# One fused attention and two MoE layers on one core: the first six weight blocks converted one VectorE stage per pair, in place of whole steps in six pairs

## The chip, the cores and the metric

The kernel runs on one core of a Trainium2 chip. The metric is the device time of one execution in microseconds (us), the median of three runs. A profile of one further execution gives a time for every instruction. Engine names are those of the profile: PE is TensorE's matmuls, PEld its weight loads, DVE is VectorE, ACT is ScalarE, POOL is GpSimd, SP is SyncE, which here issues most of the DMAs.

## The reference

```python
x = attention(q, k, v, f)        # 4 batches x 8 heads, 576 positions, 64 wide, causal, decay from log f
x = x.transpose(0, 2, 1, 3).reshape(2304, 512)
h = x @ w_in                     # 512 -> 2048
x = (maximum(h, 0) + log1p(exp(-abs(h)))) @ w_out        # softplus, 2048 -> 512
gate = 1 / (1 + exp(-(x @ w_gate)))                      # 512 -> 1536
out = (gate * (x @ w_val)) @ w_out2                      # 1536 -> 512
```

All numbers go in and come out in 32 bits. The weights lie in memory as 64-bit words (doubles), and the kernel makes of each block of 128x512 words two tiles, a high and a low part, which together carry the 32-bit value through the matmuls.

## The kernel before, in words

Attention comes first. The 32 heads are worked two at a time, so there are 16 **pairs**, 0 to 15. For each pair PE makes nine tiles of scores (L209, L220) in PSUM; DVE adds the mask and finds each row's extreme ("minimum", L227), which frees the scores' PSUM; ACT takes the exponential (L232); PE transposes the result through PSUM tiles `t` (L250); ACT copies the high part of each `t` tile out (`evac_h`, L268) and DVE the low part (`evac_l`, L272), which frees the tile; PE multiplies with the values (L322); ACT and DVE take the sums out (L332, L337), and POOL scales them (L340). POOL also splits the next queries, keys and values into high and low parts (L160, L168: `Xh`, `Yh`, `Xl`, `Yl`, `V`). DVE makes the reciprocal of each pair's row sums (L278, L279), PE turns it (`rt`, L284).

There are two `t` tiles and two score tiles `s`, used in turn. The groups of transposes of a pair follow each other on PE in the order 0, 1, 2, 3, `rt`, 5, 4, 6, and then the next pair's 0, each in the `t` tile that the last but one group left. So group 2 waits for `evac_l` of group 0, group 3 for that of group 1, group 5 for that of group 3, the next pair's group 0 for that of group 4, and its group 1 for that of group 6.

No scheduler orders this. Tables give each operation a time in units of the pair's period of 9 (`WHEN`, and `START` and `END` for the first and the last pair); pair p's operations stand at 9p + that number, all are sorted, and each engine's instructions are issued in that order. Every engine works its own queue in order and waits by semaphores.

Between attention's operations the same list takes in other work (`others`). For the weights a class `Weights` converts the blocks one after the other, each through seven stages: LOAD (SP starts a DMA of 512 KB into one of four `raw` tiles, L463), SCALE (ACT, L471), SHIFT, LOW and SIGN (DVE, L485, L487, L489, each over 128x512 32-bit words in SBUF), HI (ACT, L476), LO (POOL, L479). `op(s)` issues stage s for the next block that is ready for it, `tick()` all seven, in the order SCALE, HI, LO, SHIFT, LOW, SIGN, LOAD. During attention's pairs 0 to 15 `limit` allows six blocks, 0 to 5; the other 26 follow from attention's end on, in the next layer.

Before the change `TICKS` puts eight whole ticks among the pairs. The second to the seventh (at -7.81, 1.03, 20.49, 29.25, 38.24 and 47.34) each issue SHIFT, LOW and SIGN of one block, one straight behind the other on DVE; the last issues HI and LO of block 5.

Of the kernel before, what the change touches and what calls it, by code (L numbers as in the profile page):

```python
# [21 lines left out]
class Attention:  # L22
# [13 lines left out]
    def pools(self, pool, io_pool):  # L36
        self.vp = pool("at_v", 2)
        self.pp = pool("at_p", 2)
        self.sm = pool("at_small", 3)
        self.xp = pool("at_x", 2)  # L40
        self.io = io_pool("at_io", 2)
# [663 lines left out]
class Moe2:  # L705
# [53 lines left out]
    STEPS = 10  # L759
# [176 lines left out]

TICKS = [-79.5479, -7.81, 1.0296, 20.4876, 29.246, 38.239, 47.3352, 87.6118]
LATE_TICKS = [-7.39, 35.9211, 42.3787, 45.7979, 60.2136, 64.0078, 68.4722, 70.489, 70.7365, 71.6392, 73.755, 76.4625, 83.1312, 92.4907, 95.2063, 99.2562, 116.366, 144.939, 153.168, 159.446, 198.508]  # L940
X_STEPS = [-50.0345, -24.888, -24.7421, -11.1038, -4.6076, -2.1888, 2.7229, 20.2706]
UNITS = [58.5061, 83.1125]
# [3 lines left out]
def kernel(ctx: ExitStack, tc, q, k, v, f, w_in, w_out, w_gate, w_val, w2_out, out):  # L946
# [18 lines left out]
    W = Weights(nc, stage, 4)  # L965
# [10 lines left out]
    with ExitStack() as actx:  # L976
        ioctx = ExitStack()
        right = pools(actx, side="right")
        at = Attention(nc, q, k, v, f, xT, right, ps, dr)
        at.pools(right, pools(ioctx, side="right"))  # L980
        at.begin()
        end = at.PERIOD * at.NP
        m1 = []

        def open_pools():
            ioctx.close()
            chain = pool("chain", 1, **later)
            wb = pool("wb", 1, **later)
            W.add_slots(wb, tags("b", 2 * MORE))
            W.limit = EARLY + MORE  # L990
            m1.extend([chain, Moe1(nc, FC1, x1, yT, W, chain, ps)])

        others = [(t, W.tick) for t in TICKS] + [(end + t, W.tick) for t in LATE_TICKS]
        others += [(end + t, lambda k=k: x1.step(0, k)) for k, t in enumerate(X_STEPS)]
        others += [(end - .5, open_pools)]
        others += [(end + t, lambda u=u: m1[1].unit(u, 0)) for u, t in enumerate(UNITS)]
        at.run(others)
# [131 lines left out]
```

## Time and profile before

| what | value |
|---|---|
| time, median of three runs | 1063.03 us (1062.92 to 1065.11) |
| time of the profiled execution | 1063.44 us |
| its span, first to last instruction | 1061.7 us |
| PE busy, of the span | 1027.5 us |
| DVE busy, of the span | 678.9 us |
| ACT busy, of the span | 455.2 us |
| POOL busy, of the span | 155.4 us |

The span is what the trace shows; 1.74 us of the execution's time lie around it. Attention takes the first 230 us or so, the two layers behind it the rest. Busy times are sums over the whole span, and a busy PE isn't one at its peak: which engine sets the pace of a stretch is read from that stretch.

### The profile page before, as it was taken

The numbers are of one execution on the slowest core, as the hardware profiler recorded it, in microseconds if no ns is written. First come the engines' busy times: TensorE is split into PE (matmuls) and PEld (weight loads), VectorE is DVE, ScalarE is ACT, GpSimd is POOL, SyncE is SP. The second block draws the span as 40 slices with busy tenths as digits, with TensorE's granted clock in tenths as the row PEclk, the third lists the DMA queues.
The fourth block names the chain that finished last, engine by engine and source line by source line (L and its number), as shares of the span: only waits on it lengthen the run. The fifth ranks groups of instructions, "written<-read, shape, count | busy, mean of one in ns | idle before, by whom it ended". The sixth has DMA issues, their size and how long they took to land.

```text
span 1061.7 us, 17894 instructions
## 1 busy us (share of the span) xinstructions
PE 1027.5 (97%) x6376; PEld 924.9 (87%) x6376; DVE 678.9 (64%) x1453; ACT 455.2 (43%) x989; POOL 155.4 (15%) x158
## 2 busy tenths in 40 slices
PE   4989999989999999999999999999999999999998
PEld 3767888878889999999999998999999999899997
DVE  5899999978955755745755556655655656555421
ACT  4678888866644434344343442222222222221121
POOL 7656777440000000000000000000000000000000
PEclk9999999999999999999999999999999999999999
DMA  6354454445534565564563599997887886686481
GB/s 167 94 151 128 130 145 125 130 138 183 188 128 172 197 233 178 192 236 170 193 225 126 201 358 362 341 314 248 279 262 231 288 261 230 228 296 215 141 274 63
DMA packets 129492, 218.23 MB, mean 206 GB/s; under 512 B 16174, under 2 KB 46526, under 8 KB 129404
## 3 DMA queue, kind: packets, MB, share of 16 engines
q1 hardware_dynamic: 126364, 212.08, 61.0%
q10 hardware_dynamic: 3040, 5.01, 1.4%
q8 instruction: 50, 0.82, 0.3%
q14 instruction: 38, 0.31, 0.1%
HBM read 171.21 MB, written 45.83 MB: 204 GB/s over the span
## 4 chain that ended last, share of the span: by engine, by line
PE 88%; DVE 7%; ACT 2%; issue 1%; DMA 1%; POOL 0%; ACTq 0%; SPq 0%; DVEq 0%; POOLq 0%
PE h L540 7%; PE h L541 7%; PE h L539 7%; PE s L220 5%; PE h_S L541 4%; PE h_S L539 4%; PE h_S L540 4%; PE x L322 4%; PE t L250 4%; PE h_A L539 3%; PE h_A L541 3%; PE h_A L540 3%; PE zX L900 3%; PE zX L901 2%; PE zX L902 2%; PE oY L540 2%
## 5 line engine op out<-in xcount | busy, mean ns | idle before, releaser
L541 PE MATMUL h<-xh,wi_l 128*128 128x448 f32 (+1 forms) x320 | 118.4, 370 | 0.0
L540 PE MATMUL h<-xl,wi_h 128*128 128x448 f32 (+1 forms) x320 | 118.4, 370 | 0.0
L539 PE MATMUL h<-xh,wi_h 128*128 128x448 f32 (+1 forms) x320 | 118.4, 370 | 0.0
L581 DVE TENSOR_TENSOR gl<-L,gh 128x448 fp32r<-128x448 f32 (+1 forms) x80 | 50.9, 637 | 99.4 <-ACT gh L580 88.5
L876 ACT CAST gh<-bl 128x512 fp32r<-128x512 f32 (+1 forms) x60 | 34.6, 579 | 168.6 <-DVE bl L847 141.5
L569 ACT ACTIVATE L<-h 128x448 f32<-128x448 f32 (+1 forms) x80 | 44.2, 552 | 142.3 <-PE h L541 131.1
L232 ACT ACTIVATE P<-P,m 128x128 f32<-128x128 f32 (+3 forms) x144 | 83.4, 583 | 13.1 <-DVE m L227 13.1
L540 PE MATMUL h_S<-x,ring 128*128 128x256 f32 x288 | 81.5, 283 | 0.0
L227 DVE CUSTOM_DVE_ANT_0 P<-s,mask 128x256 f32<-128x256 f32 (+3 forms) x144 | 70.7, 517 | 15.5 <-PE s L220 10.5
L539 PE MATMUL h_S<-x,ring 128*128 128x256 f32 x264 | 74.7, 283 | 0.0
L541 PE MATMUL h_S<-x,ring 128*128 128x256 f32 x264 | 74.7, 283 | 0.0
L250 PE MATMUL t<-ident,P 128*128 128x128 f32 x400 | 62.6, 293 | 7.0 <-DVE PTbl L272 4.0
L541 PEld LDWEIGHTS h<-xh,wi_l 128*128 128x128 f32 x320 | 60.1, 188 | 6.3
L539 PEld LDWEIGHTS h<-xh,wi_h 128*128 128x128 f32 x320 | 60.1, 188 | 6.3
L540 PEld LDWEIGHTS h<-xl,wi_h 128*128 128x128 f32 x320 | 60.1, 188 | 6.3
L250 PEld LDWEIGHTS t<-ident,P 128*128 128x128 f32 x400 | 47.0, 148 | 19.7 <-DVE PTbl L272 5.7
L845 ACT ACTIVATE bh<-bh 128x1024 f32<-128x1024 f32 x24 | 25.4, 1060 | 89.4 <-DVE bh L843 89.4
L681 DVE TENSOR_TENSOR l<-fw,sh 128x512 fp32r<-128x512 f32 x60 | 40.7, 686 | 35.8 <-ACT sh L680 35.7
L540 PEld LDWEIGHTS h_S<-x,ring 128*128 128x128 f32 x288 | 55.3, 192 | 0.0
L833 DVE TENSOR_TENSOR L<-h_S,L 128x256 f32<-128x256 f32 x48 | 20.3, 423 | 53.3 <-PE h_S L541 49.9
L540 PE MATMUL h_A<-x,ring 128*128 128x256 f32 x192 | 54.3, 283 | 0.0
L877 DVE TENSOR_TENSOR gl<-bl,gh 128x512 fp32r<-128x512 f32 (+1 forms) x60 | 38.0, 635 | 24.9 <-ACT gh L876 24.9
(233 smaller groups left out, 3079.5 us busy)
## 6 DMA issues: line engine op xcount, KB each, us to landing
ring<-sd_g SPq DMA_DIRECT2D x192, 256.0 KB
ring<-sd_v SPq DMA_DIRECT2D x192, 256.0 KB
raw_wi<-in_moe_w_in_dram SPq DMA_DIRECT2D x16, 512.0 KB
raw_wo<-in_moe_w_out_dram SPq DMA_DIRECT2D x16, 512.0 KB
fraw<-in_moe_w_gate_dram SPq DMA_DIRECT2D x12, 512.0 KB
fraw<-in_moe_w_out_dram SPq DMA_DIRECT2D x12, 512.0 KB
sd_g<-sh SPq DMA_DIRECT2D x24, 256.0 KB
sd_g<-l SPq DMA_DIRECT2D x24, 256.0 KB
```

Of the source, the lines that this page charges most:

```text
L220: nc.tensor.matmul(ps[h][:, 0:N], L[o], r[o, 0:N], start=j == 0, stop=j == n - 1)
L227: self.nc.vector.tensor_tensor_reduce(P, src, mask, -0.125, 3e38, op0=ALU.add, op1=ALU.min, accum_out=R["m"][:, t:t + 1])
L232: self.nc.scalar.activation(P, P, AF.Exp, bias=R["m"][:, t:t + 1], scale=-1.0, accum_out=R["sum"][:, t:t + 1])
L250: nc.tensor.transpose(ps[:, 128 * n:128 * n + 128], R["P"][:, o:o + 128], self.ident)
L322: nc.tensor.matmul(R["acc%d" % h][:, o:o + n], v, t[:, col:col + n], start=j == 0 and w == 0, stop=j == 1 and w == 1)
L539: nc.tensor.matmul(ps, ah, bh, start=start and i == 0, stop=False)
L540: nc.tensor.matmul(ps, ah, bl, start=False, stop=False)
L541: nc.tensor.matmul(ps, al, bh, start=False, stop=stop and i == n - 1)
L569: nc.scalar.activation(g, ph, AF.Softplus)
L581: nc.vector.tensor_sub(gl, s, gh)
L681: nc.vector.tensor_sub(l, w[n], h)
L877: nc.vector.tensor_sub(l, s, h)
```

## The change

The eight ticks among the pairs go; in their place stand 44 single stages of the same six blocks. The late ticks, from 144 - 7.39 on, stay as they are, and each finds the same blocks done as before.

```diff
-TICKS = [-79.5479, -7.81, 1.0296, 20.4876, 29.246, 38.239, 47.3352, 87.6118]
+STEPS = [(-7.81, 0), (1.294, 1), (3.294, 2), (12.294, 3), (14.294, 0), (21.294, 4), (22.794, 5), (24.294, 6),
+         (28.294, 1), (30.294, 2), (39.294, 3), (41.294, 0), (48.294, 4), (49.794, 5), (51.294, 6), (55.294, 1),
+         (57.294, 2), (66.294, 3), (68.294, 0), (75.294, 4), (76.794, 5), (78.294, 6), (82.294, 1), (84.294, 2),
+         (86.294, 0), (87.381, 3), (93.294, 4), (94.794, 5), (96.294, 6), (100.294, 1), (102.294, 2),
+         (104.294, 0), (105.381, 3), (111.294, 4), (112.794, 5), (114.294, 6), (118, 0), (118.294, 1),
+         (120.294, 2), (123.381, 3), (129.294, 4), (130.794, 5), (132.294, 6), (133, 0)]
...
-        others = [(t, W.tick) for t in TICKS] + [(end + t, W.tick) for t in LATE_TICKS]
+        others = [(t, lambda k=k: W.op(k)) for t, k in STEPS] + [(end + t, W.tick) for t in LATE_TICKS]
```

The second number of a step is the stage: 0 LOAD, 1 SCALE, 2 SHIFT, 3 LOW, 4 SIGN, 5 HI, 6 LO. Worked through in order, the steps put SHIFT of block 0 into pair 0, LOW into pair 1, SIGN into pair 2, SHIFT of block 1 into pair 3, and so on: one DVE stage in each of pairs 0 to 14, always at 9p + 3.294, right behind the minimum of tiles 1 and 7. From block 3 on a block has two pairs and not three, so its LOW stands as a second DVE stage at 9p + 6.381 of pairs 9, 11 and 13. SCALE stands in pairs 0, 3, 6, 9, 11 and 13, HI and LO in pairs 2, 5, 8, 10, 12 and 14.

On DVE, in pair 2, ahead of the minimum of tiles 0 and 8, the kernel before has a whole tick (`w_wi` and `w_wo` are a block's words, `raw` its loaded doubles, the two rows of tiles `s_1` the minimum of tiles 1 and 7, `t_2` and `t_3` the transposed groups 2 and 3):

```order
L272 TENSOR_TENSOR PTal_168<-t_1_478,PTah_167 128x512
L485 TENSOR_SCALAR w_wi_532<-w_wi_532 128x512
L487 SCALAR_TENSOR_TENSOR w_wi_532<-raw_wi_316,w_wi_532 128x512
L489 SCALAR_TENSOR_TENSOR w_wi_532<-raw_wi_316,w_wi_532 128x512
L227 ISA P_437,m_438<-s_1_0_519,mask 128x256
L227 ISA m_438 128x1
L227 ISA P_437,m_438<-s_1_1_520,mask 128x256
L227 ISA m_438 128x1
L272 TENSOR_TENSOR PTbl<-t_2_550,PTbh 128x512
L272 TENSOR_TENSOR PTbl<-t_3_557,PTbh 128x2x256
```

The same place of the changed kernel:

```order
L272 TENSOR_TENSOR PTal_168<-t_1_466,PTah_167 128x512
L227 ISA P_425,m_426<-s_1_0_507,mask 128x256
L227 ISA m_426 128x1
L227 ISA P_425,m_426<-s_1_1_508,mask 128x256
L227 ISA m_426 128x1
L489 SCALAR_TENSOR_TENSOR w_wi_300<-raw_wi_255,w_wi_300 128x512
L272 TENSOR_TENSOR PTbl<-t_2_527,PTbh 128x512
L272 TENSOR_TENSOR PTbl<-t_3_535,PTbh 128x2x256
```

The tick's three stages ahead of the minimum are gone; one stage, SIGN of an older block, stands behind it, ahead of `evac_l` of groups 2 and 3.

On DVE, in pair 9, around the minimum of tiles 6 and 2 (`s_2`) and `evac_l` of groups 5 and 4 (`t_5`, `t_4`), the kernel before has no stage:

```order
L227 ISA P_1806,m_1807<-s_2_1_1978,mask 128x384
L227 ISA m_1807 128x1
L272 TENSOR_TENSOR PTbl<-t_5_1965,PTbh 128x2x256
L227 ISA P_1806,m_1807<-s_2_0_1977,mask 128x384
L227 ISA m_1807 128x1
L272 TENSOR_TENSOR PTbl<-t_4_1972,PTbh 128x384
```

The same place of the changed kernel:

```order
L227 ISA P_1775,m_1776<-s_2_1_1954,mask 128x384
L227 ISA m_1776 128x1
L272 TENSOR_TENSOR PTbl<-t_5_1939,PTbh 128x2x256
L227 ISA P_1775,m_1776<-s_2_0_1953,mask 128x384
L227 ISA m_1776 128x1
L487 SCALAR_TENSOR_TENSOR w_wo_1864<-raw_wo_1559,w_wo_1864 128x512
L272 TENSOR_TENSOR PTbl<-t_4_1946,PTbh 128x384
```

LOW of block 3 has come in ahead of `evac_l` of group 4; pairs 11 and 13 read alike.

## Rows read from the trace of the kernel before

**Rows 1.** The chain of work that ended last, pieces in order: start, us, what.

```profile
48.21 1.49 PE t L250 x7
...
62.71 0.98 PE t L250 x7
...
77.18 1.62 PE t L250 x7
...
92.82 0.98 PE t L250 x7
...
104.52 0.89 PE t L250 x7
...
116.16 0.89 PE t L250 x7
```

**Rows 2.** Busy time by stretch: a pair without a tick, one with block 5's LO.

```profile
115.90:127.50 11.60, 11.60 (x97) 9.78 (x96) 10.69 (x30) 10.09 (x30) 7.93 (x7) 1.00 0.46 128
...
139.10:150.70 11.60, 11.60 (x97) 9.78 (x96) 10.15 (x30) 10.51 (x31) 8.64 (x8) 1.00 0.55 150
```

**Rows 3.** Timeline of DVE, the tick in pair 2: start, us, instruction, idle before.

```profile
42.23 1.29 DVE L485 TENSOR_SCALAR w_wi<-w_wi 128x512 uint32<-128x512 uint32 x1
43.56 1.65 DVE L487 SCALAR_TENSOR_TENSOR w_wi<-raw_wi,w_wi 128x512 uint32<-128x512 uint32 x1
45.24 0.69 DVE L489 SCALAR_TENSOR_TENSOR w_wi<-raw_wi,w_wi 128x512 uint32<-128x512 uint32 x1
```

**Rows 4.** Timeline of POOL, the same stretch.

```profile
41.67 1.57 POOL L168 TENSOR_TENSOR V<-vr,V 128x640 fp32r<-128x640 f32 x1
43.19 1.48 POOL L479 TENSOR_TENSOR wo_l<-w_wo,wo_h 128x512 fp32r<-128x512 f32 x1
```

**Rows 5.** All instructions of line L485: count, ns min/median/max, starts.

```profile
L485 DVE TENSOR_SCALAR w_wi<-w_wi x16: 414/422/1498, 21.0 to 300.0; 128x512 uint32<-128x512 uint32 x16
```

**Rows 6.** Timeline of ACT, first pair: the first copy out of a transposed group.

```profile
22.31 0.59 ACT L268 CAST PTbh<-t 128x512 fp32r<-128x512 f32 x1 [0.29 <-PE t L250]
```

**Rows 7.** Timeline of PE, first and second pair: idle before, and what ended it.

```profile
25.82 1.97 PE L250 MATMUL t<-ident,P 128*128 128x128 f32 x8 [2.69 <-DVE PTbl L272]
...
46.33 0.92 PE L220 MATMUL s<-Yh,Xh 64*128 64x256 f32 x2 [1.74 <-DVE m L227]
```

**Rows 8.** Timeline of DVE, first pairs: `evac_l` behind the second tick, the next minimum.

```profile
29.55 0.68 DVE L272 TENSOR_TENSOR PTal<-t,PTah 128x512 fp32r<-128x512 f32 x1
...
30.75 0.74 DVE L227 CUSTOM_DVE_ANT_0 P<-s,mask 128x576 f32<-128x576 f32 x1
```

**Rows 9.** Timeline of DVE, a pair without a tick.

```profile
107.94 0.56 DVE L272 TENSOR_TENSOR PTbl<-t,PTbh 128x384 fp32r<-128x384 f32 x1
...
111.01 0.94 DVE L278 TENSOR_SCALAR r<-sum 128x9 f32<-128x9 f32 x1
...
114.50 1.29 DVE L272 TENSOR_TENSOR PTbl<-t,PTbh 128x512 fp32r<-128x512 f32 x2 [0.44 <-ACT PTbh L268]
```

**Rows 10.** Timeline of POOL, the same pair.

```profile
107.57 1.58 POOL L168 TENSOR_TENSOR Xl<-qr,Xh 128x640 fp32r<-128x640 f32 x1
...
112.69 1.56 POOL L168 TENSOR_TENSOR V<-vr,V 128x640 fp32r<-128x640 f32 x1
```

**Rows 11.** Timeline of PE, the same pair.

```profile
109.68 1.09 PE L250 MATMUL t<-ident,P 128*128 128x128 f32 x8
...
115.88 0.28 PE L284 MATMUL rt<-ident,r 128*9 128x128 f32 x1
```

**Rows 12.** Timeline of DVE, a later pair: a long reciprocal step.

```profile
192.37 1.35 DVE L278 TENSOR_SCALAR r<-sum 128x9 f32<-128x9 f32 x1
```

**Rows 13.** The chain again: groups 2 and 3, a plain pair's, then the later pair's.

```profile
171.26 1.02 PE t L250 x8
...
194.61 1.20 PE t L250 x8
```

**Rows 14.** Busy time by stretch: PE, PEld, DVE, ACT, POOL, then the granted clock.

```profile
77.40:80.80 3.40, 3.40 (x17) 2.63 (x16) 1.92 (x5) 2.81 (x9) 0.64 (x1) 0.50 0.46 95
```

## The prediction

> **What bounds the kernel now.** The page's totals call PE busy nearly throughout, but they average over stages, so I went to the chain of work in order of time. In attention it meets the same spot once per pair, the seven transposes of groups 5 and 4. Their starts are 48.21, 62.71, 77.18, 92.82, 104.52 and 116.16 [rows 1], so the pairs take 14.50, 14.47, 15.64, 11.70 and 11.64 us. The three long ones hold a tick each. The busy times of a pair without one say what sets its pace: PE 11.60 of 11.60 us, DVE 10.69, ACT 10.09, POOL 7.93 [rows 2]. So a plain pair is PE's, and DVE has 0.91 us to spare in it.
>
> A tick does not fit into that. Its three DVE stages take 1.29 + 1.65 + 0.69 = 3.63 us [rows 3]; less the 0.91 that leaves 2.7, and the pairs show 14.50 - 11.64 = 2.86. In a tick's pair DVE sets the pace and PE waits. The pair of 15.64 holds something more: from 77.40 on, for 3.4 us, the granted clock is 0.50 [rows 14], the lower of the two levels, 1.2 GHz; at half rate 3.4 us do the work of 1.7.
>
> Why does a tick take 3.63? SIGN, when POOL is idle, takes 0.69 [rows 3], and the median of all SHIFTs is 0.42 [rows 5]. In the tick, POOL's split of V ends at 41.67 + 1.57 = 43.24 and SHIFT at 43.52; POOL's LO ends at 44.67 and LOW at 45.21 [rows 3, 4]. So a stage that meets a POOL instruction waits for it and is done 0.28 (SHIFT) or 0.54 (LOW, SIGN) behind its end.
>
> The Trainium skill has this as a rule ("SBUF — State Buffer", section "Who interferes with whom"): VectorE and GpSimd share a pair of ports under an exclusive lock, and an instruction that needs the pair while the other engine holds it waits for the whole of that other instruction. The trace agrees: the 0.28 and 0.54 us are counted from the end of POOL's instruction. As an estimate by that rule, a LOW that comes just as POOL's split of the queries begins would cost the split and itself, 1.58 + 0.69 = 2.3 us [rows 3, 10], where the tick's LOW shows 1.65; for the three second LOWs the gain below would be about 2 us smaller. The rule speaks against the second LOW and hardly against the first slot, where POOL is nearly done.
>
> **The change, part by part.** All of it lies in attention, whose end I take to move with its pairs.
>
> *Removed, startup.* Two ticks stand ahead of the first pair's end. PE waits 2.69 us for the first `evac_l` and goes on at 25.82 [rows 7]. ACT's copy ahead of that `evac_l` is done at 22.31 + 0.59 = 22.90 [rows 6]; with the 0.68 that an `evac_l` takes here [rows 8], PE could start near 23.6, 2.2 us sooner. The second tick holds the next `evac_l` to 29.55, and the minimum behind it to 30.75 [rows 8]; 2.2 sooner on PE and no tick on DVE would let that minimum run at about 27.6, 3.1 sooner. PE and DVE then wait for each other, so I take 2.6, between 2.2 and 3.1.
>
> *Removed, the tick in pair 2.* PE waits 1.74 for the minimum behind it [rows 7]; a later tick costs 2.86. I take 2.4, between these.
>
> *Removed, three ticks more.* 14.50 + 14.47 + 15.64 + 11.70 less four times 11.64 is 9.8 us [rows 1]. That takes in the slow clock. Gains: 2.6 + 2.4 + 9.8 = **14.8** (13.7 to 15.7).
>
> *Added, LOW or SIGN in the slot at 3.294* (pairs 1, 2, 4, 5, 7, 8, 10, 12, 14). DVE comes free at 114.50 - 0.44 = 114.06 and then waits for ACT [rows 9]; this wait is the cover. POOL's split of V runs to 112.69 + 1.56 = 114.25 [rows 10], so the stage ends at 114.79 and `evac_l` of groups 2 and 3 starts up to 0.29 late, about 0.2 as instructions on DVE overlap a little. Behind it hangs PE: that `evac_l` ends at 115.79 and `rt` starts at 115.88 [rows 9, 11], 0.09 apart, and PE has nothing to spare. Nine times 0.2 is 1.8; from 0, if the 0.09 and what POOL does a little sooner cover it, to 0.4 each, 3.6, as pair 14 follows the tables of the end.
>
> *Added, SHIFT in the slot* (pairs 0, 3, 6, 9, 11, 13). It ends at 114.25 + 0.28 = 114.53, in time. But five of these pairs follow one with LO, 1.48 on POOL [rows 4], which pushes POOL's work later, and the reciprocal's first step, which waits for POOL too: one of 1.35 instead of 0.94 [rows 9, 12] made groups 2 and 3 take 1.20 instead of 1.02 [rows 13]. SHIFT itself meets the late split. I take 0.3 each, 1.5; from 0, since the pair with block 5's LO still took 11.60 [rows 2], to 0.6 each, 3.0.
>
> *Added, a second LOW* (pairs 9, 11, 13), ahead of `evac_l` of group 4, which starts at 107.94 [rows 9]. POOL's split of the queries runs from 107.57 to 109.15 [rows 10], so LOW ends at 109.69, and that `evac_l` at 110.2 instead of 108.50. PE wants its tile at 109.68 for the next pair's group 0 [rows 11]. What is late next is group 6's `evac_l`, behind another minimum, and with it group 1. DVE's account of such a pair is 10.69 + 0.42 + 1.7 = 12.8 against 11.60, 1.2 over; with the late LO I take 1.3, so 3.9 in all. The low end is 0.5 each, if the reciprocal's step then finds POOL between two instructions; the high end 2.4, if it meets the whole split of V, 1.56 [rows 10]. That is 1.5 to 7.2.
>
> *Costed at nothing.* ACT's SCALE and HI: ACT has 1.51 us to spare per pair, and the pair with HI of block 5, at 10.51 of ACT, still took 11.60 [rows 2]; without that cover each costs its own length, which lies in the 0.6 above. The LOADs: each stands at least 9 units, one pair, ahead of its SCALE, and its buffer came free pairs before, so SP does not wait at them, nor do the loads of q, k and v that queue behind; LOAD of blocks 6 and 7 moves late, to 118 and 133, but is wanted at 144 + 35.9.
>
> Costs: 1.8 + 1.5 + 3.9 = **7.2**. Sum: 14.8 - 7.2 = 7.6 us. The profiled span of 1061.7 becomes 1054.1; that execution took 1063.44, within 0.04% of the median, so the median becomes 1063.0 - 7.6 = **1055.4 us**, its own range 1052 to 1058.5 (chance 0.50).
>
> **The rivals.** *The late pairs hide the stages* (0.20): 10.69 + 0.69 = 11.38 is still under 11.60, so counted by engine a single stage is free, and only the second LOWs cost, 1.5 to 3. That gives a gain of 12 to 13.5, about 1050.3. Against it: the 0.09 us between `evac_l` and `rt`.
>
> *Every stage is held* (0.17): all three costs near their high ends, 3.6 + 3.0 + 6 = 12.6, because POOL, once late, stays late. Gain 2.2, about 1060.8. For it: every stage of the ticks but SIGN met POOL. Against it: POOL has 3.7 us to spare per pair.
>
> *The gain is given back at attention's end* (0.07): if the last pairs or the next layer's first weights are set by loads and not by PE, the earlier end turns into a wait; 1063. Against it: the order from 144 - 7.39 on is unchanged.
>
> *Slower, by the clock* (0.06). The short waits now fall into all pairs up to 14. If each lowers the granted clock as behind the tick at 77.40, that is 1.7 us apiece [rows 14]. It decides from five such pairs on (5 x 1.7 = 8.5 against 7.6); ten of them give 1063.0 - 7.6 + 17 = 1072. Against it: that drop lies in a tick's pair, whose waits add up to 2.9 us; of the new ones most are 0.2 and three 1.3.
>
> **How the numbers follow.** The range 1049.5 to 1061.0 takes in the main case, most of the first rival and of the second, and leaves out some 0.18. A measurement here can tell about 0.2%, 2.1 us. Faster by more: main, first rival, most of the second, 0.84; within it: the gain given back and the rest of the second, 0.09; slower 0.07, the clock and what I haven't thought of.
>
> **What would show it.** The starts of the same transposes should lie 11.6 to 12.0 apart in pairs with one stage, 12.8 to 13.2 in the three with two. LOW behind the minimum of tiles 6 and 2 should take 1.6 to 1.7 us, SHIFT in its slot under 0.7. The startup should put the first `rt` about 2.6 us sooner. The prediction is wrong if single-stage pairs stay at 11.6 to the hundredth (first rival), if they go past 12.2 (second), if the granted clock falls in late pairs, or if attention ends sooner and the end doesn't.

## The result, and the profile after

The changed kernel takes **1055.0 us** (median of 4 runs, 1051.7 to 1056.0), the kernel before, run beside it, 1063.2 (1062.9 to 1065.1): a ratio of 0.9899, 95% interval 0.9872 to 0.9926. In two later comparisons the medians were 1053.9 and 1053.1 us, the ratios 0.9904 (0.9878 to 0.9929) and 0.9890 (0.9859 to 0.9921). The profiled execution took 1055.97 us, with a span of 1054.2 us. Forecast were 1055.4 us, in a range of 1049.5 to 1061.0.

The first thing to look at is again the chain of work, at the seven transposes of groups 5 and 4, once per pair (start, us, what; compare [rows 1]):

```profile
42.77 0.98 PE t L250 x7
...
54.70 0.95 PE t L250 x7
...
66.37 0.90 PE t L250 x7
...
78.00 0.90 PE t L250 x7
...
89.86 0.89 PE t L250 x7
...
101.49 0.90 PE t L250 x7
...
113.11 0.92 PE t L250 x7
...
124.95 0.89 PE t L250 x7
...
137.77 0.89 PE t L250 x7
```

The long pairs of before (14.50, 14.47, 15.64 us) are gone: the fourth start is 78.00, where before it was 92.82. From there the pairs take 11.86, 11.63, 11.62, 11.84 and 12.82. The last one holds two stages. `rt` (L284), which stands just ahead, gives the same picture for every kernel, so all experiments below are measured by its 16 starts:

| us | before | after |
|---|---|---|
| first `rt` | 39.0 | 36.1 |
| intervals 1 to 5 | 8.84, 14.34, 14.47, 15.64, 11.96 | 6.21, 12.13, 11.68, 11.63, 11.86 |
| intervals 6 to 10 | 11.64, 11.60, 11.60, 11.60, 11.60 | 11.62, 11.63, 11.84, 12.82, 11.84 |
| intervals 11 to 15 | 11.60, 11.72, 11.81, 11.23, 11.10 | 12.77, 12.17, 12.02, 11.53, 11.10 |
| last `rt` | 219.7 | 208.9 |
| from there to the end of the span | 842.0 | 845.3 |

An interval here is the time from one `rt` to the next. Attention ends 10.8 us sooner and the kernel only 7.5 us: 3.3 us are lost behind attention. That is the first puzzle. The second is inside attention, where the new costs are smaller than forecast.

By stretch (PE, PEld, DVE, ACT, POOL, granted clock, DMA share, GB/s; compare [rows 2]) three intervals of the changed kernel, one with SHIFT behind an LO, one with LOW alone, one with two stages:

```profile
77.67:89.56 11.89, 11.85 (x98) 9.80 (x94) 11.60 (x32) 11.10 (x32) 9.21 (x8) 1.00 0.46 134
89.56:101.18 11.62, 11.62 (x96) 9.83 (x94) 11.29 (x32) 10.10 (x30) 7.94 (x7) 1.00 0.53 148
...
124.67:137.49 12.82, 11.88 (x96) 9.80 (x95) 12.64 (x33) 10.21 (x30) 8.38 (x7) 1.00 0.57 156
```

In the second PE is busy for all of 11.62 us: a single stage is hidden. In the last DVE is busy for 12.64 of 12.82 us: DVE sets that pair's pace, PE waits.

The startup, timeline of PE (idle before, and what ended it; compare [rows 7]):

```profile
23.66 1.97 PE L250 MATMUL t<-ident,P 128*128 128x128 f32 x8 [0.55 <-DVE PTbl L272]
...
30.84 0.73 PE L220 MATMUL s<-Yh,Xh 64*128 64x256 f32 x2 [0.51 <-DVE m L227]
```

The first wait has fallen from 2.69 to 0.55 us, and PE goes on at 23.66, 2.2 us sooner, as worked out (23.6). How soon the first `rt` comes varies from execution to execution, though: from 34.7 to 37.0 us in the seven profiles that have the changed startup, from 38.8 to 39.6 in the five that have the one before.

The slot with LOW, timeline of DVE, and of PE at `rt` behind it (compare [rows 9, 11]):

```profile
99.32 0.82 DVE L487 SCALAR_TENSOR_TENSOR w_wi<-raw_wi,w_wi 128x512 uint32<-128x512 uint32 x1
...
100.07 1.27 DVE L272 TENSOR_TENSOR PTbl<-t,PTbh 128x512 fp32r<-128x512 f32 x2
...
101.21 0.28 PE L284 MATMUL rt<-ident,r 128*9 128x128 f32 x1
```

LOW is held a little by POOL (0.82 instead of 0.69), yet `rt` waits for nothing. It starts at 101.21 while the second of the two `evac_l` still runs (to 101.34): it hangs on the first alone.

The pair with SHIFT, timelines of POOL and DVE (compare [rows 9, 10]):

```profile
78.90 1.30 POOL L479 TENSOR_TENSOR wo_l<-w_wo,wo_h 128x512 fp32r<-128x512 f32 x1 [2.79 <-ACT wo_h L476]
80.17 0.73 POOL L160 TENSOR_SCALAR Xh<-qr 128x640 fp32r<-128x640 f32 x1
...
84.41 1.45 POOL L340 TENSOR_TENSOR xs<-xs,rb 128x576 f32<-128x576 f32 x1
...
91.58 0.73 POOL L160 TENSOR_SCALAR Xh<-qr 128x640 fp32r<-128x640 f32 x1 [3.39 <-PE s L220]
...
84.47 1.42 DVE L278 TENSOR_SCALAR r<-sum 128x9 f32<-128x9 f32 x1
```

POOL's LO ends as Xh starts: Xh comes 2.45 us behind `rt` (77.72), where in the interval without LO it comes 1.99 behind (91.58 against 89.59). POOL is some 0.46 late from there on, and L278 is held to the end of POOL's `xs` (85.89 and 85.86): 1.42 us instead of 0.94.

The second LOW of pair 9, timelines of DVE, POOL and PE:

```profile
128.37 1.76 DVE L487 SCALAR_TENSOR_TENSOR w_wo<-raw_wo,w_wo 128x512 uint32<-128x512 uint32 x1
...
128.00 1.58 POOL L168 TENSOR_TENSOR Xl<-qr,Xh 128x640 fp32r<-128x640 f32 x1
129.53 1.87 POOL L168 TENSOR_TENSOR Yl<-kr,Yh 128x576 fp32r<-128x576 f32 x1
...
130.74 0.63 PE L250 MATMUL t<-ident,P 128*128 128x128 f32 x4 [0.58 <-DVE PTbl L272]
131.72 0.66 PE L250 MATMUL t<-ident,P 128*128 128x128 f32 x4 [0.35 <-DVE PTbl L272]
```

LOW meets POOL's split of the queries and ends 0.55 us behind it; PE's transposes wait 0.58 and 0.35 us for the evictions behind LOW.

### The profile page after: what moved, and what is told of

Read it like the earlier page. It is cut to its first block, busy times and chain, and to the rows that moved or that the text cites. A ratio compares the mean times of both kernels' runs of the same rounds, so it can differ in the third digit from the quotient of the medians.

```text
span 1054.2 us, 17893 instructions
## 1 busy us (share of the span) xinstructions
PE 1027.0 (97%) x6376; PEld 920.4 (87%) x6376; DVE 672.3 (64%) x1453; ACT 454.8 (43%) x989; POOL 154.8 (15%) x158
## 4 chain that ended last, share of the span: by engine, by line
PE 91%; DVE 5%; ACT 2%; issue 1%; DMA 0%; POOL 0%; ACTq 0%; SPq 0%; DVEq 0%; POOLq 0%
PE h L541 7%; PE h L540 7%; PE h L539 7%; PE s L220 5%; PE t L250 4%; PE x L322 4%; PE h_S L541 4%; PE h_S L539 4%; PE h_S L540 4%; PE h_A L539 3%; PE h_A L541 3%; PE h_A L540 3%; PE oY L541 3%; PE oY L540 3%; PE oY L539 3%; PE zX L900 3%
## 5 line engine op out<-in xcount | busy, mean ns | idle before, releaser
L581 DVE TENSOR_TENSOR gl<-L,gh 128x448 fp32r<-128x448 f32 (+1 forms) x80 | 51.0, 638 | 104.9 <-ACT gh L580 104.8
L876 ACT CAST gh<-bl 128x512 fp32r<-128x512 f32 (+1 forms) x60 | 34.7, 580 | 168.9 <-DVE bl L847 141.8
L250 PEld LDWEIGHTS t<-ident,P 128*128 128x128 f32 x400 | 44.7, 144 | 21.5 <-DVE PTbl L272 5.2
```

The costliest lines, as they stand in the source:

```text
L250: nc.tensor.transpose(ps[:, 128 * n:128 * n + 128], R["P"][:, o:o + 128], self.ident)
L581: nc.vector.tensor_sub(gl, s, gh)
```

## The experiments

Two theories of the smaller costs stood against each other. *Place*: a stage costs what POOL makes of it and what cover its place has. *Count*: a stage in a full pair costs its own length wherever it stands. And for the 3.3 us lost behind attention: something that differs from execution to execution, or an effect of the change.

**The two kernels unchanged, once more** (three runs, no edit).

> The changed kernel once more, nothing edited. Theory: attention is 11.2 us shorter than in the kernel before in every execution (start of rt15 near 209 us against 219.7), and what varies from execution to execution is the pace of the 448-column matmuls of the first MoE (202.7 or 206.7 ns apart, token tile by token tile, about 1.5 us a tile). Then times lie between 1051.5 (no slow tile) and 1056.2 us (three), and the profiled execution's time goes with its number of slow tiles. Rival: the slow pace comes with the change, by how the weights or the tiles lie in time after it; then tiles 2, 3 and 4 are at 206.7 ns again in this profile and the median is 1055 to 1056 us.

> The kernel before once more, nothing edited. Theory (the pace of the first MoE's matmuls is a state of the execution): a profile of it can show tiles at 206.7 ns too, and its times spread over 1062.9 to about 1067 us; the attention part is equal to the first profile's within 0.2 us. Rival (the slow pace belongs to the change): every tile is at 202.7 ns and the time stays at 1062.9 to 1063.5 us.

> The changed kernel once more, nothing edited, beside the improved one. Both theories of the improved kernel need its time on this chip: 1052 to 1056 us median, attention's intervals as in its two earlier profiles within 0.1 us, and again some token tiles of the first MoE at 206.7 ns a matmul, others at 202.7. If the slow pace belonged to the change and not to the execution, the same tiles as in the first profile (2, 3 and 4) would be slow.

The first MoE works the 2304 positions in token tiles, one of 512 and four of 448, with 384 matmuls each. The matmuls of the 448-column tiles start either 202.7 or 206.7 ns apart. By stretch, 60 us of such a tile each: the changed kernel's first profile (both stretches at 206.7), then its third (202.7), then the second profile of the kernel before (202.7, then 206.7):

```profile
380.00:440.00 60.00, 60.00 (x292) 54.49 (x291) 35.37 (x65) 24.79 (x45) 0.00 (x0) 1.00 0.55 188
...
540.00:600.00 60.00, 60.00 (x292) 54.49 (x292) 31.18 (x57) 24.42 (x45) 0.00 (x0) 1.00 0.47 161
```

```profile
540.00:600.00 60.00, 60.00 (x298) 55.61 (x297) 32.84 (x62) 25.50 (x47) 0.00 (x0) 1.00 0.50 172
```

```profile
380.00:440.00 60.00, 60.00 (x298) 55.59 (x297) 34.80 (x63) 25.68 (x47) 0.00 (x0) 1.00 0.57 198
460.00:520.00 60.00, 60.00 (x293) 54.48 (x292) 33.76 (x61) 24.86 (x45) 0.00 (x0) 1.00 0.58 202
```

With DVE, ACT and DMA about equally busy and the clock granted in full, a 60 us stretch holds 298 matmuls or some 292. Once slow, the stream stays slow for the rest of these tiles (but the last 12 matmuls, which come 5 us behind the others). The changed kernel had some three tiles, one and none at the slow pace in its three profiles; the kernel before none and two. From the last `rt` to the end the changed kernel took 845.3 us with three and 841.3 with none: 4.0 us, 1.3 a tile. (With one it took 844.1; there the granted clock was 0.50 for 6.8 us from 209.6 on, too.) So the slow pace needs no change, and the change doesn't always bring it: it belongs to the execution. Of all twelve profiles nine show it, six of the eight with single stages and three of the four without. With no slow tile the changed kernel took 1050.6 us.

Where the pace changes can be read from the traces: always at one of three places, near matmul 313, 697 or 1081 of the 1536, some four fifths into a tile, where PE's weight load waits for DVE's low part `gl` (L581). In the changed kernel's first profile, timeline of PEld:

```profile
368.19 0.19 PEld L540 LDWEIGHTS oX<-gl,wo_h 128*128 128x128 f32 x1 [0.29 <-DVE gl L581]
```

At other times the same wait passes and the pace stays. Why it changes at one and not at another is open.

Attention is reproduced: from first to last `rt` 172.8, 173.2 and 172.8 us in the changed kernel, 180.7 and 180.4 in the one before. The times spread further than the slow tiles were expected to spread them: the changed kernel's from 1051.0 to 1058.5 us (expected 1051.5 to 1056.2), the kernel before's up to 1071 (expected 1067). The start of the first `rt` is one thing more that varies; and the kernel before's second profile holds, beside those at 77.4 and 220.8, one more stretch at the lower clock, at 647 us.

**The second LOW earlier, behind the `xs` operations** (DVE's, L337, which take the sums out).

```
-(86.294, 0), (87.381, 3), ... (104.294, 0), (105.381, 3), ... (123.381, 3)
+(86.294, 0), (86.3, 3),   ... (104.294, 0), (104.3, 3),   ... (122.3, 3)
```

> The changed kernel with the second LOW of pairs 9, 11 and 13 issued some 1.6 us earlier, right behind the two xs operations of VectorE, before GpSimd's Xl and Yl start. Theory: those two pairs take 12.8 us because the stage is held by GpSimd (1.76 us instead of 0.69) and then holds the transposes; issued ahead of GpSimd's Xl it takes 0.7 to 0.8 us and the two pairs fall from 12.8 to about 11.9 us each; attention ends 1.5 to 2 us earlier and the median goes from 1055 to about 1053.3 us. Rival: VectorE has no slack between minimum 6 and the transposes' eviction, so that any second stage in the pair costs its own length; then the pairs stay at 12.4 us or more and attention gains under 0.8 us.

The two intervals fell from 12.82 and 12.77 to 12.34 and 12.29, neither 11.9 nor clearly the rival's. Timelines of DVE and POOL:

```profile
127.62 1.16 DVE L487 SCALAR_TENSOR_TENSOR w_wo<-raw_wo,w_wo 128x512 uint32<-128x512 uint32 x1
...
127.51 0.72 POOL L160 TENSOR_SCALAR Xh<-qr 128x640 fp32r<-128x640 f32 x1 [3.40 <-PE s L220]
128.20 1.11 POOL L160 TENSOR_SCALAR Yh<-kr 128x576 fp32r<-128x576 f32 x1
```

LOW had met POOL again, now at Xh, and ended 0.55 us behind it. The place was not clear of POOL, so this could not decide. The median, 1053.4 us against 1053.9 in the same comparison, can't either.

**The second LOW in a place where POOL is idle**, behind minimum 8 (pairs 9 and 11; 85.8 and 103.8 in the table).

> The changed kernel with the second LOW of pairs 9 and 11 issued behind minimum 8, ahead of the two xs operations, where GpSimd has nothing to do for over 3 us (in the run with LOW behind the xs operations it was held to 0.54 us past the end of GpSimd's Xh and took 1.16 us, and the pairs took 12.3 us). Theory now (a pair grows by nearly the whole length of its second stage): LOW takes 0.69 us and the two pairs 11.9 to 12.1 us each, against 12.8 in the changed kernel and 12.3 in the run behind the xs operations; attention ends 1.4 to 1.8 us earlier than in the changed kernel. Rival: the growth comes from the order of VectorE's work (xs, minimum 6 and the transposes' eviction come later by any stage ahead of them), not from the stage's length; then the pairs stay at 12.3 us.

The intervals are 11.82 and 11.81 us, 1.0 less than in the changed kernel, and from first to last `rt` it takes 171.2 us. Timeline of DVE, then the interval by stretch:

```profile
123.81 0.69 DVE L487 SCALAR_TENSOR_TENSOR w_wo<-raw_wo,w_wo 128x512 uint32<-128x512 uint32 x1
```

```profile
123.27:135.09 11.82, 11.82 (x96) 9.86 (x94) 11.56 (x33) 10.02 (x30) 7.93 (x7) 1.00 0.56 157
```

DVE is at 11.56 us and PE doesn't wait. Place is shown, against count and against the theory as it was put before the run too: a second stage unheld costs 0.2 us, not nearly its length. This run and the next were timed only twice each (1054.2 and 1052.9, then 1054.9 and 1051.2 us), which can't tell 1 or 2 us; the intervals can.

**HI ahead of the `bs` copies** (ACT's, L332), so that LO runs earlier.

```
-(22.794, 5) ... (49.794, 5) ... (76.794, 5) ... (94.794, 5) ... (112.794, 5) ... (130.794, 5)
+(21.5, 5)   ... (48.5, 5)   ... (75.5, 5)   ... (93.5, 5)   ... (111.5, 5)   ... (129.5, 5)
```

> The changed kernel with its six HI casts on ScalarE issued ahead of the bs copies instead of behind the copy of rt, some 1.4 us earlier; LO follows on GpSimd as soon as HI is done. Theory: pairs with SHIFT take 11.84 us, 0.24 more than a plain pair, because LO, in the same pair, delays GpSimd's Xh by about 0.5 us, and with it everything of GpSimd up to its xs operation, which holds VectorE's L278 (it ends with GpSimd's xs, at 85.89 and 85.86 us). With LO earlier Xh is not delayed, L278 takes 0.9 to 1.0 us instead of 1.42, and the SHIFT pairs behind an LO take 11.6 to 11.7 us; attention gains about 0.8 to 1.2 us. Rival: SHIFT itself or SCALE on ScalarE costs the 0.24 us; then the pairs stay at 11.8 us, and the HI ahead of the bs copies costs up to 0.3 us a pair.

The intervals of 11.86, 11.84, 11.84 and 12.17 became 11.64, 11.64, 11.60 and 11.72; from first to last `rt` 172.0 us. Timelines of POOL and DVE:

```profile
77.00 1.28 POOL L479 TENSOR_TENSOR wo_l<-w_wo,wo_h 128x512 fp32r<-128x512 f32 x1 [1.30 <-ACT wo_h L476]
79.31 0.72 POOL L160 TENSOR_SCALAR Xh<-qr 128x640 fp32r<-128x640 f32 x1 [1.03 <-DMA qr<-in_q_dram]
...
84.09 0.94 DVE L278 TENSOR_SCALAR r<-sum 128x9 f32<-128x9 f32 x1
```

Xh is on time, L278 back at 0.94. The 0.24 us were LO's, not those of SHIFT or SCALE, which stand where they stood. (HI moved with LO, and no run parts the two; POOL's rows speak for LO.)

**The kernel before, its three stages as one block in the change's slot**, LO first ahead of the block, then behind it.

```
-TICKS = [-79.5479, -7.81, 1.0296, 20.4876, 29.246, 38.239, 47.3352, 87.6118]
+TICKS = [-79.5479, -7.81, 1.0296, 87.6118]
+OTHER = [20.4876, 29.246, 38.239, 47.3352]
+BITS = [21.294, 30.294, 39.294, 48.294]
...
+        others += [(t, lambda: [W.op(s) for s in (W.SCALE, W.HI, W.LO)]) for t in OTHER]
+        others += [(t, lambda: [W.op(s) for s in (W.SHIFT, W.LOW, W.SIGN, W.LOAD)]) for t in BITS]
```

> The kernel before with SHIFT, LOW and SIGN (and the load behind them) of its four ticks in pairs 2 to 5 issued as one block behind minimum 7 of the same pair, the place that the change uses for its single stages; SCALE, HI and LO stay where the ticks were. Theory: the block cost 2.7 to 2.9 us a pair because it lay beside GpSimd's work and was held (3.6 us for the three); in the new place it takes about 2.1 us, of which some 0.8 us is slack, so that pairs of 14.3 to 15.6 us become 12.7 to 13.2 us, and attention ends 5 to 8 us earlier than before, about half or more of the change's gain, without spreading the stages. Rival: three stages in one pair cost the pair their whole length wherever they stand; then the pairs stay at 13.7 us or more, and the gain is under 3 us.

The second run issues only SCALE at the old places, and HI and LO 1.5 and 3 units behind the block.

> The kernel before with SHIFT, LOW, SIGN and the load of its four ticks in pairs 2 to 5 as one block behind minimum 7, as in the earlier run of that kind, and HI and LO behind the block instead of ahead of it, so that GpSimd does not run LO beside LOW. Theory (a pair grows by the length of the block less a slack of about 0.8 us, as 3.63 us gave 2.8 and 2.94 gave 2.2): the block takes about 2.0 us (SHIFT 0.6, LOW 0.69, SIGN 0.69), the pairs 12.8 to 13.0 us, plus up to 0.24 for LO, and attention ends some 7 us earlier than in the kernel before. Rival: three stages together delay something else (GpSimd's next Xh, PE's order) that one stage does not, so that pairs stay at 13.5 us or more.

The first went the rival's way in its intervals, 13.88, 13.80 and 13.80 us; attention ended 4.3 us sooner, between the rival's bound of 3 and the theory's of 5, ratio 0.9965 (0.9946 to 0.9984). Its timelines of DVE, POOL and PE say why:

```profile
57.43 1.66 DVE L487 SCALAR_TENSOR_TENSOR w_wo<-raw_wo,w_wo 128x512 uint32<-128x512 uint32 x1
59.12 0.69 DVE L489 SCALAR_TENSOR_TENSOR w_wo<-raw_wo,w_wo 128x512 uint32<-128x512 uint32 x1
59.73 0.68 DVE L272 TENSOR_TENSOR PTbl<-t,PTbh 128x512 fp32r<-128x512 f32 x1
...
57.07 1.47 POOL L479 TENSOR_TENSOR wi_l<-w_wi,wi_h 128x512 fp32r<-128x512 f32 x1
...
60.47 0.28 PE L284 MATMUL rt<-ident,r 128*9 128x128 f32 x1 [1.75 <-DVE PTbl L272]
61.10 0.98 PE L250 MATMUL t<-ident,P 128*128 128x128 f32 x7 [0.35 <-ACT rt_sb L289]
```

Here LO itself held LOW: the block takes 2.92 us (56.81 to 59.73), and the place was not clear. In the second run LO is out of the way; DVE and PE:

```profile
56.39 0.69 DVE L487 SCALAR_TENSOR_TENSOR w_wo<-raw_wo,w_wo 128x512 uint32<-128x512 uint32 x1
57.11 0.69 DVE L489 SCALAR_TENSOR_TENSOR w_wo<-raw_wo,w_wo 128x512 uint32<-128x512 uint32 x1
...
58.46 0.28 PE L284 MATMUL rt<-ident,r 128*9 128x128 f32 x1 [0.85 <-DVE PTbl L272]
59.09 0.99 PE L250 MATMUL t<-ident,P 128*128 128x128 f32 x7 [0.34 <-ACT rt_sb L289]
```

The block takes 1.96 us, the intervals 13.04, 12.84 and 12.84, attention ends at 211.5, 8.2 us sooner than in the kernel before, and the ratio is 0.9928 (0.9899 to 0.9958). The two runs together give an account of this place: of 2.92 us PE sees 1.75, of 1.96 it sees 0.85, so some 1.1 to 1.2 us are covered; a block that outgrows the cover costs the rest and another 0.34, since `rt` comes late and PE waits for ACT's copy of it. The cover is in [rows 9, 11]: DVE's 0.44 us of waiting for ACT, and 0.70 more from the end of the *first* of the two `evac_l` (114.50 + 0.68 = 115.18) to `rt` at 115.88. `rt` takes one of the two buffers with the tag `t`, the one that the first `evac_l` frees: in the run above that one ends at 60.41 and `rt` starts at 60.47. DVE's busy time alone, 10.69 of a plain pair and the block, gives 13.61 and 12.65 us, each 0.2 short of the interval, so these two runs speak for no account against the other; that `rt` starts as the first `evac_l` ends does.

**The startup undone.**

```
+FIRST = [-79.5479, -7.81, 1.0296]
-STEPS = [(-7.81, 0), (1.294, 1), (3.294, 2), (12.294, 3), (14.294, 0), (21.294, 4), (22.794, 5), (24.294, 6),
-         (28.294, 1), (30.294, 2), (39.294, 3), (41.294, 0), (48.294, 4), (49.794, 5), (51.294, 6), (55.294, 1),
+STEPS = [(22.794, 5), (24.294, 6), (55.294, 1),
...
+        others = [(t, W.tick) for t in FIRST] + ...
```

> The changed kernel with its start undone: the steps of the first two blocks as whole ticks at the places of the kernel before, blocks 2 to 5 by single stages as in the change; pairs 1 to 5 then hold no VectorE stage. Theory: rt0 starts at 39.0 us again instead of 36.0 and the first interval takes 8.4 to 8.8 instead of 6.2 us, so that attention ends 4.3 to 5.2 us later than in the changed kernel (2.6 and 2.4 us forecast, less some 0.2 us for SHIFT of block 1). Rival: the kernel's later pairs take the delay up (VectorE or GpSimd waits for loads of q and k); then attention ends under 3 us later.

The first `rt` is at 39.6 again and the last one at 212.3, 3.4 us later than in the changed kernel: later pairs take nothing up, and that part of the rival falls. But the first interval stayed at 6.21 us. The expectation was wrong there: pair 2's tick is the one at 20.49, block 2's, which this edit doesn't bring back. Timeline of PE (compare [rows 7]):

```profile
25.00 1.97 PE L250 MATMUL t<-ident,P 128*128 128x128 f32 x8 [3.11 <-DVE PTbl L272]
```

The 3.4 us lie between the rival's 3 and the theory's 4.3. They are one pair of profiles: from 17.5 to 27.7 and from 34.6 to 38.0 us this run's granted clock was 0.50, the lower of the two levels, 1.2 GHz, and against the start of the changed kernel's third profile (34.7, with the lower clock for 6.8 us from 17.8 on) they would be 4.8. This run answers the question of LO as well: its interval 5 holds SHIFT but neither HI nor LO, and takes 11.60 us, where the changed kernel's takes 11.86.

**All improvements together**: HI early, and the second LOW of pairs 9, 11 and 13 behind minimum 8.

> The changed kernel with all that the runs pointed to: the six HI ahead of the bs copies, and the second LOW of pairs 9, 11 and 13 behind minimum 8. Theory: the intervals between rt's of 12.8, 12.8 and 12.2 to 12.4 us become 11.6 to 11.9, those of 11.84 become 11.64; attention ends 3.2 to 4.0 us earlier than in the changed kernel (rt15 near 205 us at an equal start), and the median of the time is 3 to 4 us under the changed kernel's of the same call, about 1050.5 us. Rival: the two edits gain on one another's ground (GpSimd, earlier by the one, is met by LOW again), or the loads of q and k become what pairs wait for; then attention gains under 2.5 us.

From first to last `rt` it takes 170.3 us, 2.5 less than the changed kernel beside it (2.6 and 2.9 less than in its two other profiles); that is at the rival's bound (2.5) and short of the theory's (3.2). The two edits alone gave 1.6 and 0.8 against the first profile, so they add up as far as this scatter lets one see. The intervals of 11.82 us stayed, and so did one of 12.40, which was 12.02 to 12.40 in the changed kernel's three profiles. It ends with the slot of pair 14. Timelines of POOL, DVE and PE:

```profile
180.42 1.58 POOL L168 TENSOR_TENSOR Xl<-qr,Xh 128x640 fp32r<-128x640 f32 x1
...
181.12 1.43 DVE L489 SCALAR_TENSOR_TENSOR w_wo<-raw_wo,w_wo 128x512 uint32<-128x512 uint32 x1
...
183.20 0.28 PE L284 MATMUL rt<-ident,r 128*9 128x128 f32 x1 [0.31 <-DVE PTbl L272]
183.80 0.98 PE L250 MATMUL t<-ident,P 128*128 128x128 f32 x7 [0.32 <-DVE PTbl L272]
```

By the tables of the end POOL's Xl stands beside this slot. SIGN is held to 0.55 us behind it, takes 1.43 and outgrows the cover: `rt` waits 0.31 us, and the transposes behind it wait 0.32, which falls into the interval after. In the changed kernel's three profiles this SIGN took 1.11, 1.45 and 1.33 us. The time is 1050.6 us (median of 6, 1049.7 to 1055.6; ratio to the kernel before 0.9867, interval 0.9840 to 0.9894), the changed kernel's 1053.1 (1050.6 to 1057.6). The two spreads overlap, so it is attention's 2.5 us, more than the number of the medians, that speaks for it.

## Why the prediction was right, and where it wasn't

The forecast of 1055.4 was met to 0.4 us, but so closely by luck: two errors cancel. Attention gained 3.2 us more than forecast (10.8 against 7.6), and the profiled execution lost 3.3 behind it, where some three tiles of the first MoE ran at the slow pace. Step by step, by the first profile (an interval without stages taken as in the run with the startup undone and, later on, as in the kernel before):

| term | forecast | measured |
|---|---|---|
| startup | 2.6 (2.2 to 3.1) | 2.9 |
| pair 2's tick | 2.4 (1.74 to 2.86) | 2.6 (8.84 to 6.21) |
| three ticks more | 9.8 | 9.5 |
| LOW and SIGN in the slot | 1.8 (0 to 3.6) | about 0 (-0.02 to 0.05 in each of the five intervals that hold one alone) |
| SHIFT in the slot | 1.5 (0 to 3.0) | 1.2 (0.05, 0.26, 0.24, 0.24, 0.45) |
| second LOW, with its SIGN | 3.9 (1.5 to 7.2) | 2.6 (1.22, 1.17, 0.21; the last 0.31 and 0.59 in the other profiles) |
| not forecast, last interval but one | 0 | 0.3 |
| sum, attention | 7.6 | 10.8 |

*Gains.* All three are right to 0.3 us by the first profiles. The startup differs by 2 us from execution to execution, and pair 2's tick gives 2.2 us by the kernel before's second profile (8.36 us); in its first the granted clock was at the lower level from 46.6 to 50.0 us too, which the prediction doesn't name. The third term held the long pair with the low clock. That drop was at the same place in the kernel before's second profile, and is in none of the changed kernel's three; elsewhere they have drops of their own (at 209.6, at 17.8), so the last rival, that short waits lower the clock, has nothing for it.

*LOW and SIGN in the slot* is the step that failed: "that `evac_l` ends at 115.79 and `rt` starts at 115.88, 0.09 apart, and PE has nothing to spare". The row holds two `evac_l`, and `rt` hangs on the first alone. The cover is 1.14 us instead of 0.53, and a stage of 0.82 to 0.86 fits. Only SIGN of pair 14 doesn't, which POOL holds for longer (1.11 to 1.45 us): part of the 12.02 to 12.40, and of the last interval but one, is its cost. So the first rival, that the pairs hide single stages, was right on this term. That its time (1050.3) is close to what the changed kernel takes without a slow tile (1050.6) is in part luck: it put SHIFT at nothing, which cost 1.2, and in that profile the first `rt` came 1.3 us sooner than in the first.

*SHIFT's* size and mechanism stand: the late POOL and with it L278. HI moved ahead takes it away, all but 0.04, and without LO there is nothing of it (11.60).

*The second LOW* was forecast at 1.6 to 1.7 us long and took 1.76 and 1.75, and the pairs 12.8; the third, in pair 13, met POOL at other work, took 0.97 and cost, with the SIGN of pair 14, 0.2 to 0.6. The account of DVE (12.8 busy) was the right reading for the first two. Its reason is the hold, as the place without POOL shows. The rule of the Trainium skill ("SBUF — State Buffer", section "Who interferes with whom"), that an instruction which needs the shared ports waits for the other engine's whole instruction, agrees with the trace here: LOW ended 0.55 us behind the end of Xl, and of Xh in the run behind `xs`. Its worst case, 2.3 us, didn't come, as LOW came 0.37 us into Xl. The same section says that a VectorE instruction with at most one input from SBUF, outside its two-port modes, doesn't contend; the `xs` operations of DVE, which read PSUM beside one input from SBUF, took 1.54 us beside LO and 1.53 without it, which agrees.

*Every stage is held*, the second rival, falls: POOL caught up within the pair (its Xh of the next one comes 1.99 us behind `rt` again). *The gain is given back at attention's end* falls too, though 3.3 us were lost later: the same kernel without slow tiles took 841.3 us from the last `rt` on, the kernel before 841.9.

What the prediction did not ask is how much of the gain needs the spreading. The block of three, moved to a place clear of POOL, already brings 8.2 of the 10.8 us, with the startup as before. Of these 4.3 came with the move alone, while LO still held LOW, and 3.9 more with LO out of the way: the old place and the hold were worth about the same. In neither run does the granted clock fall among the pairs, as it did at 77.4, so a part of the 4.3 is the clock's.

## What to carry to other kernels

Before a stage is put down at its own length, read which single instruction the waiting engine hangs on (a row with x2 hides it), and add up both covers, the inserting engine's idle time and the waiter's. Where two engines hold each other up, first look for a place in which the other one is idle: moving a block there, to a place with more cover, brought three quarters of what the whole change did for attention, and the spread version still had 2.5 us left of the same kind. And measure an edit in its own stretch, by one marker instruction per iteration, when the rest of the kernel varies by more than the edit brings.

## What the runs showed of the hardware that was not expected

A steady stream of 448-column matmuls, each with its weight load, ran at 202.7 or at 206.7 ns a matmul with the clock granted in full and all other engines about equally busy; the pace changed only where PE had just waited for DVE's `gl`, at one of three places in the stream, and differed between executions of one kernel. Over three tiles that is 4.0 us, or 0.4% of the time, over a third of what the change brings. DVE's integer LOW was also held by POOL's one-input cast Xh, and POOL's next cast, Yh, took 1.11 us instead of 0.68 beside it: the hold goes both ways.
